# Scale factors in single columns and on ScalarE, scores of two heads in a row, and a new plan in a fused attention and two-layer kernel

## The chip, the core and the metric

The kernel runs on one core of a Trainium2 chip. A core has five engines with instruction streams of their own: TensorE (PE, matrix products), VectorE (DVE), ScalarE (ACT), GpSimd (POOL) and SyncE (SP, which issues the transfers). The metric is the device time in microseconds (us); less is better.

## The reference

Attention over 4 batches, 8 heads, 576 positions and 64 values a head, in which a score counts only if it lies within tau of its row's maximum. Its output, 2304 tokens of 512 values, goes through two layers of 2048 hidden values with different activations.

```
scores = scale * q @ k.T
thresh = max(scores, axis=-1) - tau
scores = where(scores >= thresh, scores, -1e9)
attn = exp(scores - max(scores)); attn = attn / (sum(attn) + 1e-9)
x = (attn @ v).transpose(0, 2, 1, 3).reshape(2304, 512)
h = x @ w1_in;  g = h * tanh(log(1 + exp(h)));            x = g @ w1_out
h = x @ w2_in;  g = h * clip(h + 3, 0, 6) / 6;            out = g @ w2_out
```

## The kernel before

**Numbers in two halves.** Products are made in f16 from a high and a low half of each scaled f32 number. A matrix of weights comes as 64-bit words, in eight groups. `convert` takes a group through a chain: shifts and additions that make f32 (L566 on ACT, L574 on POOL or L576 on DVE, L582 and L587 on DVE), a maximum over the group, `group_scale` (L457 to L464, one column for each group: the power of two by which it is divided) and, after all groups, `summary` (L481 to L505: the inverse scales of several groups at once, two or eight columns wide). The sums that make low halves are lines of `sub`, L390, on DVE or POOL. A maximum over partitions (`spread`) goes through a diagonal matrix (L417 on ACT, L419 on DVE), a matmul (L422) and a maximum (L425).

**Attention.** For each pair of heads and each 128 queries, PE makes two rows of scores (s_s, L1471, on half of its rows, 64*128, in two banks), DVE their maximum (L1480), ACT the exponential (e_ex, L1490), DVE the mask (L1493), ACT and POOL the two halves p_h and p_lo (L1498, L390), a transfer transposes them, and PE multiplies by v (L1519). k is scaled at the start by `k_scaled` (kd_lk, L1408, POOL). `to_x` puts the outputs into the order of tokens (L1633, L1639).

**First layer.** `inner` makes h for blocks of 256 tokens while attention goes on (L886, he_t copied out at L935 by ACT or L937 by DVE); `first_layer` reads it back, applies the activation (L972, L975 on ACT, L981 on DVE), and multiplies by w_out (L1001). `split_sums` scales and splits y (L692 is the maximum of a block's y, L773, L756, L762, sm_zmy and yl_zhy), which is stored and loaded again as x.

**Second layer.** `second_layer` takes nine blocks of 256 tokens. For each, a line for all blocks makes xscale (L1038) and hscales (L1039, eight columns, one for each group) on DVE. Then seven products of sums of blocks in place of eight (`product`, L1074) are combined (`keep` L1092 on ACT or DVE, `plus` L1102 on DVE), the activation is applied (L1155, L1161), the result is split in a high half (gs_h, L1171 on ACT) and a low half (L390, by half of the columns on DVE and POOL), and multiplied by w_out (L1221); L1261 and L1265 add the parts, and the result is stored.

**What sets the order.** The class `Plan` orders all of it when the program is built. A task has a cost on each engine that may do it, tasks it waits for, buffers out of rings of fixed size, and a due time (`prio`, from START, STEP and the other constants at the head of the file). `run` takes, at each step, the engine whose best candidate starts first; `_candidate` picks among those that can start about then. WHO says which engines may do which kind of task. The engines then carry out their instructions in that order.

Of the kernel before, what the change touches and what calls it, by code (L numbers as in the profile page):

```python
# [47 lines left out]
STEP = 2.707  # L48
START = 3.45
PV_OFF = 2.656  # L50
V_FIRST = -2.975
FIRST_AHEAD = 4.857
PREP_AHEAD = 4.509
CONV_STEP = 1.127
CONV_AT = 5.033
LATE_STEP = 3.262
OUT_STEP = 1.134
OUT_AT = 154.337
V_AHEAD = 5.112
# [122 lines left out]
class Plan:  # L182
# [46 lines left out]
    def _start(self, task, e):  # L229
# [18 lines left out]
        return max(t, self.clock[e])

    def _candidate(self, e):  # L250
# [94 lines left out]
def fused_kernel(ctx: ExitStack, tc, q, k, v, tau, w1i, w1o, w2i, w2o, out):  # L345
# [106 lines left out]
    def group_scale(task, name, m, i, ring, after):  # L452

        top, sc = wsc[m]["top"][:, i : i + 1], wsc[m]["sc"][:, i : i + 1]
# [15 lines left out]
        return task({"dve": 0.45}, factor, [a], [], "zf" + name)  # L470

    def summary(task, m, ring, after):
# [5 lines left out]
        def inverses(e, n):  # L478
            ts = nc.vector.tensor_scalar
            s, inv = w["s"][:, n], w["is"][:, n]  # L480
            ts(s, w["sc"][:, n], 1.875, None, ALU.mult)  # L481
# [1366 lines left out]
```

## Time and profile before

| what | us |
|---|---|
| runs | 1019.13, 1015.05, 1014.83 |
| median | 1015.05 |
| the profiled execution's own time | 1014.54 |
| its span | 1012.7 |
| PE busy | 935.0 (92%) |
| DVE busy | 784.3 (77%) |
| ACT busy | 645.8 (64%) |
| POOL busy | 531.1 (52%) |

The span is the time from the first to the last instruction on the core; the rest of the execution's time lies around it. Busy shares are means over stages that differ. The stages are: 0 to 25 us, loads and first scores; 25 to 150, attention with the conversion of the first weights; 150 to 425, attention with the first layer's h beside it; 425 to 646, the rest of the attention and the first layer; 646 to 676, the passage to the second layer; 676 to 986, the second layer; 986 to 1013, its end. [...]

### The profile page before, as it was taken

The page shows a single profiled execution, that of the slowest core. Times are in us where ns is not written, and L with a number is a line of the kernel's source. Part 1 is how long each engine was busy: PE and PEld are TensorE (multiplying, and loading weights), DVE is VectorE, ACT ScalarE, POOL GpSimd, SP SyncE. Part 2 cuts the span into 40 slices and gives each one's busy share as a digit, 9 for nine tenths or more (in the row PEclk, how much of TensorE's full clock was granted, in tenths as well). Part 3 has the DMA queues.
Part 4 walks back from the last instruction along what each step waited for, and adds up shares of the span by engine and source line. Part 5 has one row for each costly group of instructions (what it writes and reads, how often), then busy time and mean ns, then how long its engine had stood idle before and what let it go on. Part 6 is the DMA issues. An engine that isn't in the chain of part 4 may idle for free. (4 is left out here: it accounts for less than half of the span.)

```text
span 1012.7 us, 25942 instructions
## 1 busy us (share of the span) xinstructions
PE 935.0 (92%) x10776; PEld 803.2 (79%) x10776; DVE 784.3 (77%) x1466; ACT 645.8 (64%) x1029; POOL 531.1 (52%) x405
## 2 busy tenths in 40 slices
PE   3568679999999999999999999969999999999996
PEld 1446457777777777888888888869999999999986
DVE  6998899887878787668989989987746746746754
ACT  4667667888778878567776878545436536435542
POOL 5578675778656666523676567544124224213332
PEclk9878779999999999999999999979999999999999
DMA  9778989999999999885656567642101101101001
GB/s 316 168 188 206 220 213 213 230 241 225 209 231 211 251 209 231 200 314 181 217 207 217 194 225 245 244 188 74 59 1 59 59 2 59 59 2 58 23 3 42
DMA packets 201654, 164.48 MB, mean 162 GB/s; under 512 B 174144, under 2 KB 174656, under 8 KB 195136
## 3 DMA queue, kind: packets, MB, share of 16 engines
q1 hardware_dynamic: 201536, 162.82, 60.1%
q8 instruction: 85, 1.39, 0.6%
q14 instruction: 33, 0.27, 0.1%
HBM read 84.28 MB, written 36.04 MB: 119 GB/s over the span
## 5 line engine op out<-in xcount | busy, mean ns | idle before, releaser
L390 POOL TENSOR_TENSOR p_ph<-e_ex,p_ph 128x128 f16<-128x128 f32 (+3 forms) x160 | 192.6, 1226 | 97.5 <-issue 69.5
L390 POOL TENSOR_TENSOR gs_h<-g_ab,gs_h 128x896 f16<-128x896 f32 x36 | 96.3, 2691 | 219.7 <-ACT gs_h L1171 219.7
L1074 PEld LDWEIGHTS <-w__h 128*128 128x128 f16 x2016 | 157.9, 99 | 7.8 <-issue 7.0
L1221 PEld LDWEIGHTS <-gs_h 128*128 128x128 f16 x1512 | 146.6, 98 | 17.8 <-DVE out_va L1265 1.4
L1493 DVE SCALAR_TENSOR_TENSOR e_ex<-s_s,thr_th,e_ex 128x576 f32<-128x576 f32 x144 | 112.1, 812 | 21.8 <-ACT thr_th L1485 16.2
L1480 DVE TENSOR_REDUCE nm_pk<-s_s 128x1 f32<-128x576 f32 x144 | 105.8, 751 | 29.5 <-PE s_s L1471 28.9
L1471 PE MATMUL s_s<-kd_lk,qs_qp 64*128 64x288 f32 x480 | 93.8, 502 | 36.8 <-DVE e_ex L1493 24.1
L1490 ACT ACTIVATE e_ex<-s_s,nm_pk 128x576 f32<-128x576 f32 x144 | 103.8, 731 | 32.2 <-DVE nm_pk L1480 30.7
L1498 ACT ACTIVATE p_ph<-e_ex 128x576 f16<-128x576 f32 x144 | 94.7, 679 | 15.8 <-DVE e_ex L1493 13.9
L1074 PEld LDWEIGHTS <-w__u 128*128 128x128 f16 x1008 | 99.5, 99 | 1.3 <-issue 1.3
L1519 PEld LDWEIGHTS <-pt_tr 128*128 128x128 f16 x2016 | 82.5, 103 | 16.7 <-issue 8.0
L1471 PEld LDWEIGHTS s_s<-kd_lk,qs_qp 64*128 64x128 f32 x480 | 46.8, 215 | 58.9 <-issue 37.8
L1519 PE MATMUL aux_pv<-vh,pt_tr 128*128 128x65 f16 (+1 forms) x1296 | 87.5, 204 | 6.1 <-DMA pt_tr<-p_ph 6.1
L1171 ACT ACTIVATE gs_h<-g_ab 128x1792 f16<-128x1792 f32 x36 | 59.9, 1691 | 35.3 <-DVE g_ab L390 34.1
L1519 PE MATMUL aux_pv<-vl_vl,pt_tr 128*128 128x64 f16 x720 | 71.5, 204 | 0.0
L1155 ACT ACTIVATE g_ab<-g_ab,aux,hscales 128x512 f32<-128x512 f32 x72 | 54.2, 804 | 20.4 <-DVE g_ab L1102 20.4
L935 ACT ACTIVATE he_t<-h_g,hin 128x512 f32<-128x512 f32 x70 | 47.8, 683 | 28.0 <-PE h_g L886 22.6
L390 DVE TENSOR_TENSOR gs_h<-g_ab,gs_h 128x896 f16<-128x896 f32 x36 | 48.0, 1334 | 17.9 <-ACT gs_h L1171 17.9
L1102 DVE TENSOR_TENSOR g_ab<-h_g0d,s_ka 128x256 f32<-128x256 f32 x36 | 13.6, 420 | 59.1 <-PE h_g0d L1074 42.0
L981 DVE SCALAR_TENSOR_TENSOR gs_h<-hp_e,fscales,gs_h 128x512 f16<-128x512 f32 x72 | 51.9, 743 | 4.6 <-ACT gs_h L975 4.4
L972 ACT ACTIVATE hp_e<-hl_l 128x512 f32<-128x512 f32 x72 | 42.3, 596 | 20.5 <-DVE gs_h L981 20.1
L975 ACT ACTIVATE gs_h<-hp_e,fscales 128x512 f16<-128x512 f32 x72 | 47.4, 683 | 7.3 <-PE y_y L1001 6.6
(677 smaller groups left out, 2628.7 us busy)
## 6 DMA issues: line engine op xcount, KB each, us to landing
hd<-he_t SPq DMA_DIRECT2D x36, 512.0 KB, 3.6
hl_l<-hd SPq DMA_DIRECT2D x18, 1024.0 KB, 5.1
raw_lr<-in_moe_w_in SPq DMA_DIRECT2D x16, 1024.0 KB, 5.5
raw_lr<-in_moe_w_out SPq DMA_DIRECT2D x16, 1024.0 KB, 6.1
yd<-yl_zhy SPq DMA_DIRECT2D x9, 896.0 KB, 4.8
qs_qp<-in_q SPq DMA_DIRECT2D x11, 576.0 KB, 6.4
v_lv<-in_v SPq DMA_DIRECT2D x16, 320.0 KB, 4.0
kd_lk<-in_k SPq DMA_DIRECT2D x16, 288.0 KB, 4.9
```

The costliest lines, as they stand in the source:

```text
L390: engine[e].tensor_tensor(dst, a, b, ALU.subtract)
L981: nc.vector.scalar_tensor_tensor(s.tile[:, k, 1], g.tile.rearrange("p (a n) -> p a n", a=2), fs[:, fp : fp + 1], s.tile[:, k, 0], ALU.mult ...
L1074: mm(dst.tile[:, i * Q : (i + 1) * Q], wt[2][fp][wl].tile[:, right - 1, c * P : (c + 1) * P], x[xl].tile[:, c, left - 1], start=first and ...
L1155: nc.scalar.activation(g.tile[:, k, 4:8], g.tile[:, k, 0:4], AF.Relu, bias=wsc[2]["aux"][:, fp : fp + 1], scale=hscale[:, fp : fp + 1],)
L1171: nc.scalar.activation(part.tile[:, :, 0], g.tile[:, :, 1:], AF.Copy)
L1221: mm(region(p), part[:, gl, left - 1], wt[3][fp][wl].tile[:, right - 1], start=fp == n == 0 and spot(p)[1] == 0, stop=fp == NG - 1 and n == 2,
L1471: mm(s[j].tile[:, half, :HALF], lh[r], rh[r], start=m == 0, stop=m == len(terms) - 1,)
L1480: nc.vector.tensor_reduce(neg.tile[:, j : j + 1], sv(j), AX.XY, ALU.max, negate=True)
L1490: nc.scalar.activation(ev(j), sv(j), AF.Exp, bias=neg.tile[:, j : j + 1])
L1493: nc.vector.scalar_tensor_tensor(ev(j), sv(j), thr.tile[:, j : j + 1], ev(j), ALU.is_ge, ALU.mult)
L1498: nc.scalar.activation(p16.tile[:, js, :S], e_.tile[:, js], AF.Copy)
L1519: mm(ov[:, dst, :d], pt.tile[:, j, ch, :], part.tile[:, src, vc, :], start=i == j == ch == 0 and part is vh, stop=j == w - 1 and ch == 8, ...
```

## The change

The power of two of a group and its inverse are now both made in `group_scale`, in single columns (for the first matrix, m = 0); `summary` does seven groups early and the last one alone, and its last step is ScalarE's. In `second_layer` xscale and hscales are made for each block behind its first product, xscale on DVE and hscales on ACT. k is scaled on ACT. All low halves of the second layer's g (`o0` and `o1`) are on DVE, as are eight low halves of weights (`u20`) that were POOL's. In `Plan`, PE stays with scores if another score row can start within STAY, and from JOIN_FROM on the first of a pair's score rows waits until two banks are free soon (JOIN), so that both heads' rows stand together. Nearly all constants of the plan have new values.

```
-STEP = 2.707
-START = 3.45
+STEP = 2.83
+START = 11.118
...
-    "c20": ("dve",), "c21": ("pool", "dve"), "c30": ("pool",), "c31": ("dve",),
-    "q2": ("pool", "dve"), "q3": ("pool",), "u20": ("pool",), "u21": ("pool",),
-    "u30": ("pool",), "u31": ("pool", "dve"), "uy0": ("pool", "dve"), "uy1": ("dve",),
-    "kh": ("pool",), "vh": ("act",), "q": ("dve",), "o0": ("dve",), "o1": ("pool",),
+    "c20": ("dve",), "c21": ("pool",), "c30": ("pool", "dve"), "c31": ("pool", "dve"),
+    "q2": ("pool", "dve"), "q3": ("pool", "dve"), "u20": ("dve",), "u21": ("pool",),
+    "u30": ("pool",), "u31": ("pool",), "uy0": ("pool", "dve"), "uy1": ("pool", "dve"),
+    "kh": ("act",), "vh": ("act",), "vl": ("dve",), "q": ("dve",), "o0": ("dve",), "o1": ("dve",),
...
+JOIN = 2.418
+JOIN_FROM = 306.548
+STAY = 0.992
...
+        if e == "pe" and task.kind == "s" and task.name[-1] == "0" and self.clock[e] > JOIN_FROM:
+            both = task.bufs[0].ring.when(2)
+            if both is None:
+                return None
+            t = max(t, both - JOIN)
...
+        if e == "pe" and self.halves:
+            more = [(s, t) for s, t in found if t.kind == "s" and s <= self.clock[e] + STAY]
+            if more:
+                return min(more, key=lambda c: (c[0], c[1].prio))
...
-        top, sc = wsc[m]["top"][:, i : i + 1], wsc[m]["sc"][:, i : i + 1]
+        top, sc, inv = (wsc[m][k][:, i : i + 1] for k in ("top", "sc", "is"))
...
+            if m == 0:
+                nc.vector.tensor_scalar_mul(inv, sc, 2.0 ** -111)
             nc.vector.tensor_scalar_mul(sc, sc, 2.0 ** -112)
+            if m == 0:
+                nc.vector.tensor_scalar(
+                    bits(inv), bits(inv), 3, INF_BITS, ALU.logical_shift_left, ALU.bitwise_and
+                )
+                nc.vector.tensor_scalar(bits(inv), bits(inv), INF_BITS, None, ALU.bitwise_xor)
...
+        def apply(e):
+            nc.scalar.activation(w["f"], w["is"], AF.Copy, scale=w["c"][:, 1:2])
+
+        some = slice(0, NG - 1)
+        early = {0: 2.5, 1: 1.5, 2: 3.5, 3: 1.5}[m]
+        a = task({"dve": early}, lambda e: part(e, some), after[:-1], [], f"zi{m}")
+        a = task({"dve": 1.0 if m % 2 else 1.6}, largest, [a, after[-1]], [], f"zs{m}")
         if m == 0:
-            step = NG // len(scaled_parts)
-            for i in range(len(scaled_parts)):
-                n = slice(i * step, (i + 1) * step)
-                scaled_parts[i] = task(
-                    {"dve": 0.7}, lambda e, n=n: inverses(e, n), after[n], [], f"zi{i}_"
-                )
-            return task({"dve": 1.6}, scales, [*after, *scaled_parts], [], f"zs{m}")
-        if m % 2 == 0:
-            return task({"dve": 2.4}, scales, after, [], f"zs{m}")
-        a = task({"dve": 0.9}, scales, after, [], f"zs{m}")
-        a = spread(task, f"s{m}", lambda: w["c"][:, 0:1], [], ring, a)
-        return task({"dve": 0.4}, rows, [a], [], f"zr{m}")
+            return a
+        if m % 2:
+            a = spread(task, f"s{m}", lambda: w["c"][:, 0:1], [], ring, a)
+            a = task({"dve": 0.31}, row_scale, [a], [], f"zr{m}")
+        return task({"act": 0.29}, apply, [a], [], f"zu{m}")
...
-            nc.vector.tensor_scalar(hscale, wsc[2]["b"], a, None, ALU.mult)
+
+        def hidden(e):
+            nc.scalar.activation(hscale, wsc[2]["b"], AF.Copy, scale=xs(blk, 0))
...
-        scaled = task({"dve": 0.4}, scales, [y_stored[blk], scaled_by["y"]], [], "zx")
-        gs, made = [], []
+        gs, made, scaled = [], [], []
...
             p1 = product(X, 1, 2, True, [], "a")
+            if u == 0:
+                a = task(
+                    {"dve": 0.16}, scales, [y_stored[blk], scaled_by["y"]], [], "zx", 0.0, 0, [p1]
+                )
+                scaled.append(a)
+                scaled.append(task({"act": 0.29}, hidden, [a], [], "zw", 0.0, 0))
...
-        kl = prep(pick("kh", act=0.65, pool=1.0), k_scaled, [lk], [kd], "kh")
+        kl = prep(pick("kh", act=0.72, pool=1.73), k_scaled, [lk], [kd], "kh")
...
-        mul(w["f"], w["f"], wsc[3]["f"], ALU.mult)
-        ts(w["f"], w["f"], 0.125, None, ALU.mult)
+        nc.vector.scalar_tensor_tensor(
+            w["f"], w["f"], 0.125, wsc[3]["f"], ALU.mult, ALU.mult
+        )
```

The order of VectorE at the passage to the second layer, before (sm_zmy0_8 is the maximum of the last block's y, hscales and xscale those of the second layer's blocks); three more pairs of L1038 and L1039 stand behind these rows:

```order
L1039 TENSOR_SCALAR hscales_126<-b2_6625,xscale_121 128x8
L692 TENSOR_REDUCE sm_zmy0_8_0_8_1_9780<-y_y00_0_0_8_0_9477 128x1
L695 TENSOR_SCALAR sm_zmy0_8_0_8_1_9780<-sm_zmy0_8_0_8_1_9780 128x1
L1038 TENSOR_SCALAR xscale_121<-xscale_121,xinv_122,scy_127 128x1
L1039 TENSOR_SCALAR hscales_126<-b2_6625,xscale_121 128x8
```

And now (L720, L723 are L692, L695 of before; L431 is the diagonal on DVE, L437 the maximum behind the matmul, L801 and L402 a part and a low half of the y of the block before):

```order
L801 SCALAR_TENSOR_TENSOR xf_zvy0_7_0_7_1_9687<-y_y00_0_0_7_0_9218,sm_zmy0_7_0_7_1_9528,xf_zvy0_7_0_7_1_9687 128x2x128 x3
L1009 SCALAR_TENSOR_TENSOR gs_h4_0_8_1_9532<-hp_e7_0_8_1_9703,fscales_125,gs_h4_0_8_1_9532 128x512
L801 SCALAR_TENSOR_TENSOR xf_zvy0_7_0_7_1_9687<-y_y00_0_0_7_0_9218,sm_zmy0_7_0_7_1_9528,xf_zvy0_7_0_7_1_9687 128x2x128
L402 TENSOR_TENSOR yl_zhy0_7_0_7_1_9741<-xf_zvy0_7_0_7_1_9687,yl_zhy0_7_0_7_1_9741 128x896
L1066 TENSOR_SCALAR xscale_121<-xscale_121,xinv_122,scy_127 128x1
L1284 TENSOR_SCALAR xscale_121<-xscale_121,scy_127 128x1
L720 TENSOR_REDUCE sm_zmy0_8_0_8_1_9830<-y_y00_0_0_8_0_9515 128x1
L723 TENSOR_SCALAR sm_zmy0_8_0_8_1_9830<-sm_zmy0_8_0_8_1_9830 128x1
L431 TENSOR_SCALAR dgb_zdy0_8_0_8_1_9862<-ident_75,sm_zmy0_8_0_8_1_9830 128x128
L437 TENSOR_REDUCE sm_zmy0_8_0_8_1_9830<-h_zpy0_8_0_8_1_9864 128x1
```

The operations on eight columns are gone from here, one xscale is left, and the chain of the last block's y stands in a row.

The order of VectorE in the early attention, where the second group of the first matrix gets its scale (sc0 the power of two, s0 and is0 the inverse), before:

```order
L460 TENSOR_SCALAR top0_146<-top0_146 128x1
L461 TENSOR_SCALAR sc0_147<-top0_146 128x1
L464 TENSOR_SCALAR sc0_147<-sc0_147 128x1
L1480 TENSOR_REDUCE nm_pk2_0_0_1_375<-s_s2_0_1_0_364 128x1
L481 TENSOR_SCALAR s0_148<-sc0_147 128x2
L482 TENSOR_SCALAR s0_148<-s0_148 128x2
L483 TENSOR_SCALAR is0_149<-s0_148 128x2
L484 TENSOR_SCALAR is0_149<-is0_149 128x2
```

And now, for the first group:

```order
L472 TENSOR_SCALAR top0_146<-top0_146 128x1
L473 TENSOR_SCALAR sc0_147<-top0_146 128x1
L477 TENSOR_SCALAR is0_149<-sc0_147 128x1
L478 TENSOR_SCALAR sc0_147<-sc0_147 128x1
L480 TENSOR_SCALAR is0_149<-is0_149 128x1
L483 TENSOR_SCALAR is0_149<-is0_149 128x1
L469 TENSOR_SCALAR top0_146<-top0_146 128x1
```

The four operations on two columns, which stood behind each second group, have gone; each group has three more on one column.

The order of PE at one query tile late in the attention (s_s14_0_0 and s_s14_0_1 are the score rows of the two heads), before:

```order
L886 LDWEIGHTS w0__h0_0__1_541
L886 MATMUL h_g00_0_0_5_1_5059<-x_fl8_2_2_4293,w0__h0_0__1_541 128x256
L1471 MATMUL s_s14_0_0_0_5064<-kd_lk14_0_4709,qs_qp14_0_4482 128x288 x2
L1639 MATMUL aux_fl11_4_1_5069<-istack_91,xtail1_144 128x64
L1471 MATMUL s_s14_0_1_0_5074<-kd_lk14_0_4709,qs_qp14_0_4482 128x288 x2
L1519 LDWEIGHTS pt_tr12_0_1_1_4945
L1519 MATMUL aux_pv12_0_0_1_5081<-vh0_134,pt_tr12_0_1_1_4945 128x65
```

And now:

```order
L914 LDWEIGHTS w0__h0_6__1_1470
L914 MATMUL h_g60_0_0_4_1_4999<-x_fl8_0_2_3618,w0__h0_6__1_1470 128x256
L1517 MATMUL s_s14_0_0_0_5076<-kd_lk14_0_4689,qs_qp14_0_4541 128x288 x2
L1517 MATMUL s_s14_0_1_0_5085<-kd_lk14_0_4689,qs_qp14_0_4541 128x288 x2
L1565 LDWEIGHTS pt_tr12_1_1_1_4983
L1565 MATMUL aux_pv12_0_0_1_5022<-vh0_134,pt_tr12_1_1_1_4983 128x65
L1565 LDWEIGHTS pt_tr12_1_1_1_4983
```

Before, a matmul that turns attention's output (L1639) stood between the two heads' scores; now they stand together. Over the whole program the stretches of score matmuls that stand in a row fall from 96 to 79.

## Rows read from the trace of the kernel before

**Rows 1.** Busy time of the engines by stage; columns: stretch, length, busy time (instructions), clock
```profile
25.00:150.00 125.00, 88.91 (x852) 63.65 (x852) 113.26 (x211) 82.91 (x146) 91.84 (x80) 0.79 0.83 199
...
425.00:646.00 221.00, 219.58 (x2018) 196.43 (x2017) 191.69 (x323) 164.69 (x243) 126.46 (x92) 1.00 0.64 225
646.00:676.00 30.00, 20.89 (x222) 19.03 (x220) 27.06 (x62) 10.03 (x14) 14.91 (x11) 0.83 0.58 217
676.00:986.00 310.00, 309.20 (x4253) 293.77 (x4250) 199.89 (x409) 150.91 (x197) 93.67 (x35) 1.00 0.12 40
```

**Rows 2.** What TensorE waited for, 0 to 150 us: total, times, longest
```profile
PE s_s L1471 <- DVE e_ex L1493: 25.8, 13, 5.2
...
PE s_s L1471 <- POOL kd_lk L1408: 7.0, 1, 7.0
```

**Rows 3.** VectorE in order of time, 33 to 38 us: start, length, operation
```profile
34.50 0.96 DVE L483 TENSOR_SCALAR is<-s 128x2 uint32<-128x2 uint32 x1
```

**Rows 4.** GpSimd in order of time, at 33 and at 665 us
```profile
33.39 2.05 POOL L574 TENSOR_TENSOR cvt_c__1_373<-cvt_c__1_373,eight 128x512 int32<-128x512 int32 x2
...
665.43 1.89 POOL L390 TENSOR_TENSOR yl_zhy<-xf_zvy,yl_zhy 128x896 f16<-128x896 f32 x1
```

**Rows 5.** Groups of instructions by shape, the whole span: busy, mean ns, idle before
```profile
L390 DVE TENSOR_TENSOR gs_h<-g_ab,gs_h 128x896 f16<-128x896 f32 x36 | 48.0, 1334 | 17.9 <-ACT gs_h L1171 17.9
...
L482 DVE TENSOR_SCALAR s<-s 128x2 uint32<-128x2 uint32 x4 | 3.2, 804 | 0.1
...
L481 DVE TENSOR_SCALAR s<-sc 128x2 f32<-128x2 f32 x4 | 2.0, 512 | 0.0
...
L460 DVE TENSOR_SCALAR top<-top 128x1 f32<-128x1 f32 x32 | 4.7, 148 | 0.4
...
L390 POOL TENSOR_TENSOR gs_h<-g_ab,gs_h 128x896 f16<-128x896 f32 x36 | 96.3, 2691 | 219.7 <-ACT gs_h L1171 219.7
...
L1408 POOL TENSOR_SCALAR kd_lk<-kd_lk,qscale 128x576 f32<-128x576 f32 x16 | 27.6, 1728 | 8.2 <-DMA kd_lk<-in_k 8.1
...
L1498 ACT ACTIVATE p_ph<-e_ex 128x576 f16<-128x576 f32 x144 | 94.7, 679 | 15.8 <-DVE e_ex L1493 13.9
...
L1102 DVE TENSOR_TENSOR g_ab<-h_g0d,s_ka 128x256 f32<-128x256 f32 x36 | 13.6, 420 | 59.1 <-PE h_g0d L1074 42.0
```

**Rows 6.** TensorE in order of time, 299.5 to 305.5 us
```profile
299.84 0.76 PE L1471 MATMUL s_s<-kd_lk,qs_qp 64*128 64x288 f32 x4
300.53 1.27 PE L886 MATMUL h_g<-x_fl,w__h__1_629 128*128 128x256 f16 x10
...
302.87 1.73 PE L1471 MATMUL s_s<-kd_lk,qs_qp 64*128 64x288 f32 x12
```

**Rows 7.** Busy time of the engines, 666 to 676 us
```profile
666.00:676.00 10.00, 6.79 (x72) 6.48 (x71) 8.22 (x24) 3.12 (x5) 3.40 (x2) 0.55 0.74 275
```

**Rows 8.** VectorE in order of time, 660.5 to 673 us
```profile
660.19 1.08 DVE L390 TENSOR_TENSOR yl_zhy<-xf_zvy,yl_zhy 128x896 f16<-128x896 f32 x1
...
663.93 1.21 DVE L692 TENSOR_REDUCE sm_zmy<-y_y 128x1 f32<-128x1024 f32 x1
...
665.55 1.79 DVE L1039 TENSOR_SCALAR hscales<-b,xscale 128x8 f32<-128x8 f32 x1
...
671.74 0.28 DVE L425 TENSOR_REDUCE sm_zmy<-h_zpy 128x1 f32<-128x128 f32 x1
```

**Rows 9.** What TensorE waited for, 646 to 676 us
```profile
PE h_zpy L422 <- ACT dgb_zdy L417: 3.4, 1, 3.4
PE h_g0d L1074 <- DVE sm_zmy L425: 2.0, 1, 2.0
```

**Rows 10.** VectorE's groups of instructions by shape, 425 to 646 us
```profile
L390 DVE TENSOR_TENSOR yl_zhy<-xf_zvy,yl_zhy 128x896 f16<-128x896 f32 x11 | 17.7, 1619 | 1.5 <-ACT yl_zhy L762 1.5
...
L576 DVE TENSOR_SCALAR cvt_c__1_9549<-cvt_c__1_9549 128x512 uint32<-128x512 uint32 x1 | 0.4, 420 | 0.0
```

More of the change, by code (lines that the diff above doesn't have):

```diff
@@ L46 @@
 RELEASE = dict.fromkeys(("s", "m", "h", "y", "aux"), 0.27)
-STEP = 2.707
-START = 3.45
[L50 to L59, printed above, removed]
+STEP = 2.83
+START = 11.118
+PV_OFF = 3.414
+V_FIRST = 5.763
+FIRST_AHEAD = 6.308
+PREP_AHEAD = 4.584
+CONV_STEP = 1
+CONV_AT = 6.827
+LATE_STEP = 1.5
+OUT_STEP = 4.268
+OUT_AT = 107.984
+V_AHEAD = 4.249
 MOE_OFF = 9.75
-MOE_LAG = 11.98
-RATE = 0.9
+MOE_LAG = 13.564
+RATE = 0.918
 NX = 3
-FLIP = 2.992
-ALPHA = {"act": 6.104, "pe": 4.357}
-FITS = 0.072
+FLIP = 3.534
+ALPHA = {"act": 5.473, "pe": 1.636}
+FITS = 0.168
 PORT = ("vl", "c", "u", "o", "zs", "q", "p")
@@ L469, in group_scale @@
             a = spread(task, name, lambda: top, [], ring, a)
[L470 removed]
+        return task({"dve": 0.97 if m == 0 else 0.5}, factor, [a], [], "zf" + name)
     def summary(task, m, ring, after):
@@ L480, in inverses, with bounds, part, largest @@
             s, inv = w["s"][:, n], w["is"][:, n]
-            ts(s, w["sc"][:, n], 1.875, None, ALU.mult)
+            ts(s, w["sc"][:, n], 2.0, None, ALU.mult)
             ts(bits(s), bits(s), 3, INF_BITS, ALU.logical_shift_left, ALU.bitwise_and)
             ts(bits(inv), bits(s), INF_BITS, None, ALU.bitwise_xor)
-            ts(inv, inv, 0.5, None, ALU.mult)
-        def scales(e):
+        def bounds(e, n):
             ts, tt = nc.vector.tensor_scalar, nc.vector.tensor_tensor
-            if m:
-                inverses(e, slice(0, NG))
+            bound = w["b"][:, n]
+            tt(bound, w["top"][:, n], w["sc"][:, n], ALU.mult)
+            ts(bits(bound), bits(bound), 3, INF_BITS, ALU.logical_shift_left, ALU.bitwise_and)
+            tt(bound, bound, w["is"][:, n], ALU.mult)
+        def part(e, n):
+            if m:
+                inverses(e, n)
+            if m % 2 == 0:
+                bounds(e, n)
+        def largest(e):
+            ts = nc.vector.tensor_scalar
+            part(e, slice(NG - 1, NG))
+            nc.vector.tensor_reduce(w["c"][:, 0:1], w["is" if m % 2 else "b"], AX.X, ALU.max)
             if m % 2:
-                nc.vector.tensor_reduce(w["c"][:, 0:1], w["is"], AX.X, ALU.max)
                 return
-            tt(w["b"], w["top"], w["sc"], ALU.mult)
-            ts(bits(w["b"]), bits(w["b"]), 3, INF_BITS, ALU.logical_shift_left, ALU.bitwise_and)
-            tt(w["b"], w["b"], w["is"], ALU.mult)
-            nc.vector.tensor_reduce(w["c"][:, 0:1], w["b"], AX.X, ALU.max)
             ts(bits(w["c"][:, 1:2]), bits(w["c"][:, 0:1]), INF_BITS, None, ALU.bitwise_xor)
@@ L554, in convert @@
             one_conversion(m, g, raw, [loaded, factors[g]], task)
+        if m == 0:
+            step = NG // len(scaled_parts)
+            scaled_parts[:] = [factors[i : i + step] for i in range(0, NG, step)]
         scaled_by[m] = summary(tasker(prio + 2 * NG * off), m, ring, factors)
@@ L849, in input_scales @@
             n = slice(part * NG // parts, (part + 1) * NG // parts)
-            after = scaled_parts[part : part + 1] if i == 0 else scaled_parts
+            after = scaled_parts[part] if i == 0 else [f for fs in scaled_parts for f in fs]
             a.append(task({"act": 0.27}, lambda e, n=n: scales(e, n), [ready, *after], [], f"zx0_{i}"))
@@ L1249, in factor_out @@
             nc.vector.tensor_scalar(xs(blk, 1), xs(blk, 0), const_y[:, 1:2], None, ALU.mult)
-        factored = task({"dve": 0.15}, factor_out, [scaled, scaled_by["out"]], [], "zo")
+        factored = task({"dve": 0.15}, factor_out, [*scaled, scaled_by["out"]], [], "zo", 0.0, NG - 1)
         side_, yo = Buf(r_out), Buf(r_out)
```

43 lines of the change are left out of this document (25 added, 18 removed).

## The prediction

> **What bounds the kernel now.** I read the stages first, then the waits of TensorE (PE), then the rows at the stalls. The profiled execution took 1014.54 us with a span of 1012.7, so 1.8 us lie around the span; the median of the runs, 1015.05, is 0.5 above it. In [rows 1] the reader is to compare PE's busy time with the length of each stage. From 425 to 646 (the rest of the attention and the first layer) PE is idle for 1.4 of 221 us, from 676 to 986 (second layer) for 0.8 of 310, at clock 1.00. There only less PE work helps. PE has room in two places: from 25 to 150, where it is idle for 36.1 of 125 us at a mean granted clock of 0.79, and from 646 to 676, the passage from layer one to layer two, where it is idle for 9.1 of 30 us at 0.83. The waits tell whom it waits for. Early it is VectorE (DVE): 25.8 us in thirteen waits for the masked exponentials (e_ex), and 7.0 us once for the first scaled k from GpSimd (POOL) [rows 2]. DVE is busy for 113.3 of those 125 us, 91%: its own work is what ends last, and any microsecond taken off it there can reach PE.
>
> Why DVE is so full shows in [rows 3, 4]: L483 handles two columns, 256 numbers, and takes 0.96 us. It ends at 35.46, and the pair of POOL additions that ran beside it ends at 35.44. L1039 (eight columns) starts at 665.55 and lasts 1.79, to 667.34; POOL's sum beside it runs to 667.32 [rows 4, 8]. So these small operations of several columns last until POOL's instruction is over. Single columns do not: L460, one column, means 148 ns over 32 instances [rows 5].
>
> **The passage.** In [rows 8] the reader is to see DVE's order from 663 on: L692 (the maximum of the last token block's y), then L1039 of the other blocks, one of them with 1.79 us, and only at 671.74 L425, which ends the maximum over partitions of that block's y. PE's waits there include 3.4 us for the diagonal dgb_zdy made from L692's result, and 2.0 us for L425 [rows 9]. [...]
>
> **The change, part by part.** The sum is against 1014.54.
>
> *A. Early stage, −4.8.* Removed: four sets of L481 to L484 on two columns, 16 operations; L481 sums to 2.0 us and L482 to 3.2 [rows 5], and L483 and L484 read like L482, in all 11.6 us. Added: three single columns for each of eight groups, 24 operations; at the pitch of about 0.19 us that such operations have in a row (an estimate from L460's 148 ns and a little issue time) 4.6 us. DVE saves 7.0 us. PE waits for e_ex for 23.5 of its 36.1 idle us in this stage, and some of DVE's work stands where nobody waits, so I take 55%, 3.8 us. The first k goes to ScalarE (ACT): L1408 takes 1728 ns on POOL; on ACT nothing of this shape was traced, the nearest row is L1498 with 576 columns, 0.68 us [rows 5]. That is 1.05 us earlier at the very start, where PE waits for it; I take 1.0. Fifteen more k add some 10 us to ACT over the attention, beside DVE's 91%. The new times by which work is due (first constants of the table) reorder everything else in this stage; bounds 0 and −8 (all of 7.0 and 1.05).
>
> [...]
>
> *B. Scores in a row, −2.7.* Score matmuls use half the rows (64*128), all others 128*128. Four of them start at 299.84 and the next other matmul at 300.53; twelve last 1.73 and four 0.76 [rows 6]. So one record costs (1.73−0.76)/8 = 0.121 us, and a stretch of them (0.69−0.48) = 0.21 beyond its records. In the order of the program the stretches fall from 96 to 79; 13 of the missing ones are in the time when PE is never idle. 13 × 0.21 = 2.7. Bounds: −3.8 with 0.08 more on entering, and +3.4 if sixteen newly joined pairs each hold PE back 0.21 us until the second bank is free.
>
> *C. Passage, −10.5.* No L1039 is left on DVE. A block's xscale (one column) is made behind that block's first products, its eight hidden scales on ACT. In the new order L720 (L692 before) follows the first block's xscale directly, and its diagonal is made on DVE behind it, with no queue. What is late next is the chain itself: maximum 1.21 and L437's 0.28 [rows 8], the diagonal on 128 columns (by the 1.08 us for 896 columns it takes at most that) and the hops between them, about 3 us. PE's order has two other products ahead of its matmul. I leave 1.5 us, half of the chain, for it and for the load of the x columns. Bounds −6 (part of the clock loss stays) and −12.
>
> *D. First layer, +1.5.* DVE takes eight low halves of weights (128x768, from POOL) and five more he_t copies, and gives eight shifts (L576) to POOL. An operation of two inputs on 128x896 takes 1.08 us undisturbed [rows 8], so 768 columns take 0.93: 7.4. Five copies at 0.68 (ACT's row for 576 columns, the nearest) are 3.4. Eight shifts at 0.42 [rows 10] are −3.4. DVE goes from 191.7 to about 199 of 221 us. PE idles 1.4 us with DVE at 87%, so I take a fifth, 1.5. Bounds: 0, and +11.7 if all of 7.4 reaches PE and every low half is stretched by 0.54 as the yl_zhy of this stage are (1.62 against 1.08) [rows 8, 10].
>
> *E. Second layer, 0.* All 36 low halves that POOL did in 2.69 us go to DVE (1.08 undisturbed, 1.33 mean) [rows 5]. DVE rises from 199.9 by at least 38.9 to 239 of 310 us. PE's operand is ready 1.4 us earlier. What hides it is DVE's idle time: ahead of L1102 alone 59.1 us over 36, 1.64 each, 42.0 of it spent waiting for PE's own products [rows 5]. If that cover is gone, each costs up to 1.08. Bounds 0 and +5.
>
> The other edits (one operation instead of two for the combined scales, seven columns early and one late for each weight's sums, f on ACT, factor_out by block) are short operations off PE's path in [rows 1]'s full stages, except at the passage, where C has them: 0.
>
> Sum: −4.8 −2.7 −10.5 +1.5 +0 = −16.5, to 998.0; with the 0.5 between this execution and the median, **998.5**.
>
> **Rivals.**
> R1, *only the passage is gained.* PE's early idle time is bound by the order of the chain score, peak, exponent, mask rather than by DVE's total, and the joined scores move waits about. For it: the single longest waits for e_ex last 5.2 us [rows 2], more than any L48x. Against: 91% busy. A and B are nothing: −10.5+1.5 = −9.0, 1006.
>
> R2, *DVE becomes the bound of the first layer.* For it: yl_zhy is already stretched by half [rows 10]. Against: POOL has less to do afterwards. D at its upper bound: −16.5−1.5+11.7 = −6.3, 1008.7. [...]
>
> R3, *the other side: the low halves on DVE hold PE's evacuations.* In the second layer PE's banks are emptied by DVE and ACT; a low half of 1.08 us ahead of L1131 (L1102 before) delays g, the activation and the next output. Full price 36 × 1.08 = 38.9: 1037. It makes the kernel slower than before by over 0.5% once more than 21.6 of the 38.9 us (0.6 us each) land on PE. For it: PE has no idle time there, so every delay shows. Against: 1.64 us idle ahead of each L1102.
>
> R4, *the passage still stalls.* The chain of the last block's y stays late because the operations of the block before (L801, L402) stand ahead of its maximum on DVE, and the clock falls again. C is nothing: −6.0, 1009.
>
> **How the numbers follow.** The forecast case (990 to 1003.5) has 0.45; R1 0.18; R2 0.10; R4 0.12; R3 0.11; better than 990, 0.04. The low end of the range is A, B and C at their bounds, −8 −3.8 −12, with D 0: 990.7, taken as 990. The high end takes in R1, R2 and most of R4: 1011; R3, the tail under 990 and a part of R4 are left out, 2 in 10. The measurement can tell about 0.5%, 5 us, from no change: to 1010.0 is faster. All of the forecast case, R1, the tail, and nearly all of R2 and half of R4 are faster: 0.78. The rest of R4 and R2, and half-strength R3, are the same: 0.12. R3 beyond 0.6 us each is slower: 0.10.
>
> **What would show it.** A: PE idle from 25 to 150 near 31 us, waits for e_ex about 21 to 22 us; the new single columns at 0.15 us beside POOL's work. B: fewer and longer score stretches, PE busy 2 to 3 us less in 150 to 646. C: no DVE operation of eight columns in the passage, PE idle below 2 us in the 30 us around it, mean granted clock there above 0.95. D: PE idle in the first layer about 3 us. E: PE busy in every slice of the second layer, DVE near 235 to 240. I am wrong if idle time from 25 to 150 stays at 36 (R1), if PE waits for gs_h or h_g there (R2), if waits on DVE appear in the second layer (R3), or if dgb_zdy or sm_zmy still lead the waits of the passage (R4).

## The result and the profile after

The changed kernel took 991.62 us (median of 990.03, 990.23, 993.0 and 994.76) against 1015.52 us for the kernel before in the same comparison: ratio 0.9761, 95% interval 0.9725 to 0.9798. That is 23.9 us less; 17 were forecast, in a range that holds 991.62 near its low end. The profiled execution (990.03, the fastest of the four) has a span of 988.3 us, 24.4 less than before.

Busy time by stage of the changed kernel, columns as in [rows 1]; the clock is the granted one of PE as a share of its full speed. A stage of the same name now holds later work, since everything stands some 11 to 24 us earlier:

```profile
25.00:150.00 125.00, 91.79 (x929) 64.40 (x925) 114.76 (x237) 93.99 (x167) 90.84 (x82) 0.84 0.92 221
425.00:646.00 221.00, 220.02 (x2035) 197.24 (x2033) 195.26 (x340) 162.77 (x243) 143.00 (x101) 1.00 0.64 229
646.00:676.00 30.00, 30.00 (x504) 29.57 (x502) 25.17 (x57) 18.68 (x26) 2.54 (x2) 1.00 0.49 177
```

From 646 to 676 PE is now full at clock 1.00, and so it is in the 30 us around its own passage (632.6 to 662.6); before, the passage had 9.1 us idle at 0.83, and from 666 to 676 PE was busy for 6.79 us at a mean clock of 0.55 [rows 7]. By an estimate from these two numbers, 6.79 × 0.45, some 3 us of them are the clock's, which with the idle time makes about 12 us. From 25 to 150 PE is still idle for 33.2 us, but it carries out 929 instructions instead of 852, at 0.84 instead of 0.79. In the second layer (the same length of 310 us, 18 us earlier) GpSimd does nothing and VectorE about 30 us more:

```profile
658.00:968.00 310.00, 308.67 (x4193) 292.71 (x4191) 229.84 (x459) 152.42 (x205) 0.00 (x0) 1.00 0.12 39
```

Where the time came from is read from PE's milestones. Of the kernel before, the last product of the attention and the first of the second layer:

```profile
422.88 0.40 PE L1519 MATMUL aux_pv<-vh,pt_tr 128*128 128x130 f16 x4
...
658.34 0.22 PE L1074 MATMUL h_g0a<-xl_x__1_0_0_9309,w__h 128*128 128x128 f16 x1
```

And of the changed kernel:

```profile
411.67 0.40 PE L1565 MATMUL aux_pv<-vh,pt_tr 128*128 128x130 f16 x4
...
644.91 0.22 PE L1103 MATMUL h_g0a<-xl_x__1_0_0_9351,w__h 128*128 128x128 f16 x1
```

The attention ends 11.2 us earlier; up to the first product of the second layer it is 13.4 us. Between these two marks PE carries out the same 384 products of h and 1728 of y in both kernels. The ends differ by 24.4, and behind the start of the second layer nothing more is gained or lost: from the 303rd of its products to the end both kernels take 326.4 us. So, in these two executions: attention −11.2, first layer −2.2, passage −11.0, second layer 0.

VectorE at the passage, changed kernel (the answer to [rows 8]):

```profile
633.06 1.22 DVE L615 SCALAR_TENSOR_TENSOR cvt_c__1_9458<-raw_lr,cvt_c__1_9458 128x1024 uint32<-128x1024 uint32 x1
...
643.04 0.21 DVE L1284 TENSOR_SCALAR xscale<-xscale,scy 128x1 f32<-128x1 f32 x1
645.11 1.22 DVE L720 TENSOR_REDUCE sm_zmy<-y_y 128x1 f32<-128x1024 f32 x1 [1.85 <-PE y_y L1029]
...
646.56 0.29 DVE L431 TENSOR_SCALAR dgb_zdy<-ident,sm_zmy 128x128 bf16<-128x128 f32 x1
647.85 0.29 DVE L437 TENSOR_REDUCE sm_zmy<-h_zpy 128x1 f32<-128x128 f32 x1 [1.00 <-PE h_zpy L434]
```

The last conversion of weights (L615) is over at 634.28, 10.6 us ahead of the first product. L720, the maximum of the last block's y, waits for nothing but PE, and L437 ends 3.0 us behind its start; it was 8.1 us, from 663.93 to 672.02 [rows 8].

What PE waits for up to 150 us, and the operations that the change made (the answers to [rows 2, 5]; the last two rows are ScalarE's):

```profile
PE s_s L1517 <- DVE e_ex L1539: 34.5, 19, 5.5
PE s_s L1517 <- ACT kd_lk L1441: 5.8, 1, 5.8
```

```profile
L402 DVE TENSOR_TENSOR gs_h<-g_ab,gs_h 128x896 f16<-128x896 f32 x72 | 74.4, 1087 | 15.6 <-ACT gs_h L1206 15.6
...
L502 DVE TENSOR_SCALAR is<-s 128x7 uint32<-128x7 uint32 x3 | 2.3, 756 | 0.1
...
L477 DVE TENSOR_SCALAR is<-sc 128x1 f32<-128x1 f32 x8 | 1.2, 154 | 0.3
...
L1441 ACT ACTIVATE kd_lk<-kd_lk,qscale 128x576 f32<-128x576 f32 x16 | 12.3, 771 | 4.2 <-DMA kd_lk<-in_k 4.1
...
L1069 ACT ACTIVATE hscales<-b,xscale 128x8 f32<-128x8 f32 x9 | 2.6, 292 | 0.4 <-DVE xscale L1066 0.4
```

The eight single columns of L477 take 153 to 156 ns, and each of them began while GpSimd was at work; seven columns (L502) take 756 on average. The low halves of g take 1.09 us on VectorE now that GpSimd does nothing beside them; those of [rows 5] took 1.33, and with GpSimd back on half of them (a_lo_on_pool, below) VectorE's half takes 1.52.

### The profile page after: what moved, and what is told of

It is laid out like the page before. It is cut to its first block, busy times and chain, and to the rows that moved or that the text cites. A ratio compares the mean times of both kernels' runs of the same rounds, so it can differ in the third digit from the quotient of the medians.

```text
span 988.3 us, 25879 instructions
## 1 busy us (share of the span) xinstructions
PE 921.7 (93%) x10776; PEld 796.0 (81%) x10776; DVE 790.4 (80%) x1512; ACT 651.6 (66%) x1054; POOL 407.4 (41%) x354
## 4 chain that ended last, share of the span: by engine, by line
PE 69%; DMA 5%; DVE 2%; issue 1%; ACT 0%; SPq 0%; DVEq 0%; ACTq 0%
PE y_y L1029 17%; PE h_g L914 11%; PE hp_g1a L1103 5%; PE h_g0a L1103 5%; DMA pt_tr<-p_ph 4%; PE s_s L1517 3%; PE aux_pv L1565 3%; PE hp_g1d L1103 2%; PE h_g0d L1103 2%; PE h_g1b L1103 1%; PE hp_g0b L1103 1%; PE y_y__1_8_0_15084 L1256 1%; PE y_y___1_0_0_10340 L1256 1%; PE y_y___1_7_0_14653 L1256 1%; PE y_y___1_6_0_13984 L1256 1%; PE y_y___1_5_0_13325 L1256 1%
## 5 line engine op out<-in xcount | busy, mean ns | idle before, releaser
L402 POOL TENSOR_TENSOR p_ph<-e_ex,p_ph 128x128 f16<-128x128 f32 (+3 forms) x160 | 189.0, 1203 | 119.6 <-issue 72.0
L1517 PE MATMUL s_s<-kd_lk,qs_qp 64*128 64x288 f32 x480 | 88.2, 480 | 41.7 <-DVE e_ex L1539 32.2
L1539 DVE SCALAR_TENSOR_TENSOR e_ex<-s_s,thr_th,e_ex 128x576 f32<-128x576 f32 x144 | 112.0, 811 | 15.1 <-ACT thr_th L1531 12.8
L1565 PEld LDWEIGHTS <-pt_tr 128*128 128x128 f16 x2016 | 80.4, 102 | 18.8 <-DMA pt_tr<-p_ph 10.4
L402 DVE TENSOR_TENSOR gs_h<-g_ab,gs_h 128x896 f16<-128x896 f32 x72 | 74.4, 1087 | 15.6 <-ACT gs_h L1206 15.6
L963 ACT ACTIVATE he_t<-h_g,hin 128x512 f32<-128x512 f32 x65 | 44.4, 684 | 22.7 <-PE h_g L914 15.5
L1196 DVE SCALAR_TENSOR_TENSOR g_ab<-g_ab,f 128x512 f32<-128x512 f32 x72 | 51.2, 747 | 5.0 <-ACT g_ab L1190 5.0
L1121 ACT ACTIVATE s_ka<-h_g0a 128x512 f32<-128x512 f32 x27 | 16.1, 596 | 49.5 <-PE h_g0a L1103 49.3
```

What stands on the lines that cost most here:

```text
L402: engine[e].tensor_tensor(dst, a, b, ALU.subtract)
L1517: mm(s[j].tile[:, half, :HALF], lh[r], rh[r], start=m == 0, stop=m == len(terms) - 1,)
L1539: nc.vector.scalar_tensor_tensor(ev(j), sv(j), thr.tile[:, j : j + 1], ev(j), ALU.is_ge, ALU.mult)
L1565: mm(ov[:, dst, :d], pt.tile[:, j, ch, :], part.tile[:, src, vc, :], start=i == j == ch == 0 and part is vh, stop=j == w - 1 and ch == 8, ...
```

## Experiments

Kernels whose name begins with b are the kernel before with an edit, those with a the changed one. Where it says that the order is kept, every engine has its instructions in the same order but for the edited ones. Each was timed against the kernel before; the changed kernel stands at 0.9761 on this scale, and 0.001 is 1.0 us.

**b_hscales_act.** The eight-column scales on ScalarE, where they stood.
```
-            nc.vector.tensor_scalar(hscale, wsc[2]["b"], a, None, ALU.mult)
+            nc.scalar.activation(hscale, wsc[2]["b"], AF.Copy, scale=a)
```


> The kernel before, its order kept; only the eight-column hscales of each second-layer block are made on ScalarE instead of VectorE, at the same place. My account (the queue of L1039 ahead of and behind the last block's maximum is the passage's stall): the passage gains most of its 12 us, so 8 to 11 us less in all. Rival (the order by block, not the engine, removed the stall, since the scales still all stand early and wait on the stores): 0 to 3 us less.


Measured 0.9973 (0.9960 to 0.9986), 2.7 us less: the rival's number, for another reason than its. Its waits of PE in the passage, and ScalarE's order there:

```profile
PE h_g0a L1074 <- ACT s_ka L1092: 3.1, 1, 3.1
...
PE h_zpy L422 <- ACT dgb_zdy L417: 0.9, 1, 0.9
```

```profile
663.18 0.66 ACT L1039 ACTIVATE hscales<-b,xscale 128x8 f32<-128x8 f32 x3
665.01 1.06 ACT L642 ACTIVATE st_h<-sum_h 128x1024 f16<-128x1024 f32 x1 [1.17 <-POOL sum_h L390]
665.97 0.58 ACT L1092 ACTIVATE s_ka<-h_g0a 128x512 f32<-128x512 f32 x1
```

The wait for dgb_zdy fell from 3.4 to 0.9 us, as my account had it, but the wait for the first copy of the second layer (s_ka) grew from 1.2 to 3.1 us. The copy starts at 665.97, behind the high half of the last group of weights (L642), which GpSimd's sum held until 665.01.

**b_hscales_by_block.** As above, and the scales of blocks 1 to 8 only ahead of each block's first activation.
```
-            nc.scalar.activation(hscale, wsc[2]["b"], AF.Copy, scale=a)
+            todo.append(lambda: nc.scalar.activation(hscale, wsc[2]["b"], AF.Copy, scale=a))
+            if blk == 0:
+                todo.pop()()
...
                 def relu(e, k=k, fp=fp):
+                    while todo:
+                        todo.pop()()
```


> The kernel before, its order kept, hscales on ScalarE and those of blocks 1 to 8 only ahead of each block's first activation (L1155), as the change does. If eight small operations in ScalarE's queue are what held the first copy of the second layer: 3 us less than b_hscales_act, 0.994. If the last weights' conversion holds it: the same as b_hscales_act, 0.997.


Measured 0.9975 (0.9958 to 0.9992), as b_hscales_act, and the wait for the copy is still there:

```profile
PE h_g0a L1078 <- ACT s_ka L1096: 3.4, 1, 3.4
```

So it is not the number of scales in ScalarE's queue that holds it, and the order by block, the rival of the run before, adds nothing here.

**b_hscales_act_keep_dve.** As b_hscales_act, the first copy on VectorE.
```
-                    if e == "act":
+                    if e == "act" and (blk, u, tag) != (0, 0, "a"):
```


> The kernel before, its order kept, hscales on ScalarE as in b_hscales_act, and the copy of the first product of the second layer (s_ka, L1092) on VectorE instead of ScalarE. In b_hscales_act PE still waited 3.1 us for that copy, which stood behind the high half of the last group of weights (L642), itself held until 665.01 by GpSimd's sum. If late conversions of weights are what remains of the passage's stall: 3 to 6 us less than b_hscales_act, ratio to the kernel before 0.991 to 0.994. Rival (something else is next, the last block's maximum or the x columns): no further gain, 0.997.


Measured 0.9953 (0.9933 to 0.9973), 4.7 us less than before and 2 less than b_hscales_act; the intervals overlap, and the time lies between the two accounts. In its trace PE is busy for all of the 10 us from 666 to 676 at clock 1.00, but later it waits 2.5 us for x columns of the next block:

```profile
PE h_g0a L1074 <- DMA xl_x__1_1_0_10071<-yd: 2.5, 1, 2.5
```

**b_single_columns.** The inverse scales of the first matrix column by column, 32 operations for 16; the order is kept.
```
+            for k in range(n.start, n.stop) if m == 0 else (n,):
+                c = slice(k, k + 1) if m == 0 else k
-            s, inv = w["s"][:, n], w["is"][:, n]
+                s, inv = w["s"][:, c], w["is"][:, c]
...
```


> The kernel before, its order kept; only the four inverse scales of the first matrix are made column by column (32 operations on one column for 16 on two). My account: VectorE saves about 5.5 us (11.6 less 32 times 0.19) between 25 and 150 us and PE gains about half, 3 us. Rival (VectorE's total is not what sets the pace there, the new order is): 0 to 1 us.


Measured 0.9921 (0.9908 to 0.9934): 8.0 us less (6.7 to 9.3), more than either account. The 16 operations took 11.5 us; 32 at the pace of b_three_edits below (eight in 1.25 us) take 5.0, so VectorE saves some 6.5 us by this estimate.

**b_k_on_act.** k on ScalarE; the order is kept.
```
-            if e == "act":
-                nc.scalar.activation(kd.tile, kd.tile, AF.Copy, scale=qscale)
-            else:
-                nc.gpsimd.tensor_scalar(kd.tile, kd.tile, qscale, None, ALU.mult)
+            nc.scalar.activation(kd.tile, kd.tile, AF.Copy, scale=qscale)
```


> The kernel before, its order kept; only k is scaled on ScalarE instead of GpSimd. My account: 1.0 us less at the start, nothing after, since ScalarE has room. Rival: ScalarE's queue delays exponentials early and up to 3 us are lost again.


Measured 0.9990 (0.9972 to 1.0009), not told from nothing. Its waits say why: the wait for k is 1.2 us shorter than in [rows 2], and the next, for the scale of v, which was 5.2 us, is 1.0 us longer.

```profile
PE s_s L1468 <- DVE vs_ve L1356: 6.2, 1, 6.2
PE s_s L1468 <- ACT kd_lk L1405: 5.8, 1, 5.8
```

**b_three_edits.** b_hscales_act, b_single_columns and b_k_on_act together.


> The three edits above together in the order of before. If they add up by my account: 12 to 15 us less, more than half of the 24 us that the change brought. If the new plan is what gained: under 6 us.


Measured 0.9891 (0.9873 to 0.9910): 11.1 us less, nearly half of what the change brought; alone the three make 2.7 + 8.0 + 1.0 = 11.7. What a column count does is best seen at one place of the traces. VectorE of the kernel before, and PE's next scores:

```profile
101.71 0.68 DVE L481 TENSOR_SCALAR s<-sc 128x2 f32<-128x2 f32 x1
102.42 1.08 DVE L482 TENSOR_SCALAR s<-s 128x2 uint32<-128x2 uint32 x1
103.54 1.08 DVE L483 TENSOR_SCALAR is<-s 128x2 uint32<-128x2 uint32 x1
104.66 0.96 DVE L484 TENSOR_SCALAR is<-is 128x2 f32<-128x2 f32 x1
105.53 1.53 DVE L1493 SCALAR_TENSOR_TENSOR e_ex<-s_s,thr_th,e_ex 128x576 f32<-128x576 f32 x2
```

```profile
106.48 3.25 PE L1471 MATMUL s_s<-kd_lk,qs_qp 64*128 64x288 f32 x12 [3.51 <-DVE e_ex L1493]
```

VectorE of b_three_edits at the same place (first two and last of eight single columns, and the masks):

```profile
97.21 0.14 DVE L483 TENSOR_SCALAR s<-sc 128x1 f32<-128x1 f32 x1
97.38 0.15 DVE L484 TENSOR_SCALAR s<-s 128x1 uint32<-128x1 uint32 x1
...
98.38 0.15 DVE L486 TENSOR_SCALAR is<-is 128x1 f32<-128x1 f32 x1
98.46 1.53 DVE L1492 SCALAR_TENSOR_TENSOR e_ex<-s_s,thr_th,e_ex 128x576 f32<-128x576 f32 x2
```

Before, 3.8 us pass from L481 to the masks, and PE waits 3.51 us for them; its twelve score matmuls then take 3.25 us, against 1.73 for twelve in [rows 6]; the granted clock in these 3.2 us is 0.50. Now the eight operations take 1.25 us, and PE's wait for the masks at this place is gone. Over the first 150 us the waits for e_ex fall from the 25.8 us of [rows 2] to 14.8:

```profile
PE s_s L1470 <- DVE e_ex L1492: 14.8, 7, 3.6
```

**a_extra_two_columns** and **a_extra_one_column.** The changed kernel, order kept, with three more operations on a spare tile in each of eight group scales; their results are not used. Shown is the run with two columns; the other has `0:1` for `0:2`.
```
...
+                for k in range(3):
+                    nc.vector.tensor_scalar(
+                        bits(spare[:, 0:2, 0]), bits(spare[:, 0:2, 0]), INF_BITS, None, ALU.bitwise_xor
+                    )
```


> The changed kernel, its order kept, with three more operations on two columns of a spare tile in each group scale of the first matrix (24 in all; they compute nothing that is used). If two columns beside GpSimd's work cost 0.8 us each and all of it is on the path of the masks: 19 us slower than the changed kernel, more if the clock falls. If half of it is: 10 us. If the price of a column count is not what mattered: as with one column, below 3 us.

> The same with three more operations on one column of the spare tile (24 in all). At 0.19 us each VectorE has 4.6 us more: 2 to 5 us slower than the changed kernel if the path is VectorE's, near 0 if not.


Measured 0.9923 (0.9898 to 0.9949) and 0.9805 (0.9782 to 0.9827): 16.4 and 4.5 us over the changed kernel, 12.0 apart. The interval of the one-column run overlaps the changed kernel's, so its 4.5 us alone are not told from nothing. The groups of VectorE with two columns, then with one:

```profile
L488 DVE TENSOR_SCALAR spare<-spare 128x2 uint32<-128x2 uint32 x24 | 14.4, 602 | 0.6
```

```profile
L488 DVE TENSOR_SCALAR spare<-spare 128x1 uint32<-128x1 uint32 x24 | 3.6, 151 | 0.6
```

The second column costs VectorE 14.4 − 3.6 = 10.8 us, and the kernel 12.0, give or take some 3 by the two intervals. So these microseconds count about in full. The 602 ns are a mean over 24. How far such an operation depends on GpSimd shows in the kernel before, in its sixteen on two columns (L481 to L484): with GpSimd idle beside them three took 0.17 us each; of the thirteen with GpSimd at work eleven took 0.68 to 1.08, the other two 0.16 and 0.49.

**a_lo_on_pool.** The changed kernel, order kept, 36 low halves of g back on GpSimd.
```
-                sub(e, part.tile[:, k, 1], g.tile[:, k, 1:], part.tile[:, k, 0])
+                sub("pool" if k else e, part.tile[:, k, 1], g.tile[:, k, 1:], part.tile[:, k, 0])
```


> The changed kernel, its order kept, with the second low half of each pair in the second layer back on GpSimd (36 of 72). By term E nothing: within 1 us. If GpSimd's 2.7 us each delayed PE: several us slower.


Measured 0.9787 (0.9764 to 0.9810); the interval overlaps the changed kernel's, so no difference is shown. GpSimd takes 2.9 us for each, and PE waits for none of them. From the 303rd product of the second layer to the end its profiled execution takes as long as the changed kernel's, within 0.01 us:

```profile
L402 POOL TENSOR_TENSOR gs_h<-g_ab,gs_h 128x896 f16<-128x896 f32 x36 | 103.7, 2895 | 213.1 <-ACT gs_h L1206 199.0 <-PE y_y___1_7_1_14654 L1256 14.1
```

**a_no_join_no_stay** and **a_no_join.** The changed kernel, planned anew without both rules (STAY at −1e9, JOIN_FROM at 1e9), and without JOIN alone.
```
-JOIN_FROM = 306.548
-STAY = 0.992
+JOIN_FROM = 1e9
+STAY = -1e9
```


> The changed kernel, planned without the two rules that put scores together (JOIN and STAY off, all other numbers the same). By the forecast's term B it loses 2.7 us (ratio to the kernel before near 0.979). Rival: the joined scores bring nothing, since PE waited more in the attention after the change; then within 1 us of the changed kernel (0.976), or faster.


Measured 1.0045 (1.0026 to 1.0065): 29 us slower than the changed kernel, which neither account had. The longest waits of PE that the changed kernel does not have:

```profile
PE h_g0a L1103 <- DMA xl_x__1_0_0_9806<-yd: 9.3, 1, 9.3
PE aux_fl L1685 <- DVE xtail L1656: 8.2, 1, 8.2
```

The planner put the x columns and a turn of attention's output elsewhere. This prices the plan, not the scores: the run is no measure of term B. Nor does it bring the old order of scores back: in its trace they stand in 82 stretches, where the changed kernel has 79 and the kernel before 96.


> The changed kernel planned without JOIN alone; the order is the same up to the middle of the attention. By term B the rest of the attention is about 2 us longer up to the last score row. Rival: the joined rows gain nothing there, since the first row waits for the second bank as long as the stretches save; within 1 us at the last score row. What the plan does behind the attention (conversions, passage) may differ and is read apart.


Measured 0.9798 (0.9772 to 0.9824), 3.8 us over the changed kernel with overlapping intervals. In its profiled execution the last score row is 6.6 us later than in the changed kernel's, but 6.1 of them were there already at the first place where the orders differ (309.95 us against 303.8). Its scores stand in 79 stretches too, so the run does not test term B, which prices fewer stretches.

**b_three_edits_late_off.** b_three_edits with one number of the plan, which converts the last weights earlier.
```
-OFF_LATE = 1.875
+OFF_LATE = 4.862
```


> The kernel of b_three_edits with one number of the plan changed, OFF_LATE from 1.875 to 4.862 as in the changed kernel. The order is the same up to the start of the first layer; from there the last group of weights is converted earlier (17 VectorE rows ahead of the last block's maximum, before 6), the hidden scales are done before it, and no conversion is left in the passage. If the late conversions are the other part of the passage's 12 us: 6 to 8 us less than b_three_edits, ratio to the kernel before 0.981 to 0.983. If the earlier conversions cost the first layer what they give, or the passage has another stall: 0.987 to 0.990.


Measured 0.9948 (0.9931 to 0.9966), slower than b_three_edits by 5.8 us. That is worse than either account: the rival, too, expected no more than 0.990. My account was right on the place, the rival on where it would be lost. In its trace the first product of the second layer starts at 662.68, and the passage behind it is nearly full, at clock 1.00:

```profile
662.00:680.00 18.00, 17.62 (x309) 17.42 (x308) 9.30 (x24) 8.74 (x15) 1.16 (x1) 1.00 0.44 157
```

But PE's longest wait from 400 us on now stands in the first layer, for a block's scale (L697) at 619.83. On VectorE a conversion of 3.13 us, which GpSimd held back by 0.94, and more of the same group stand ahead of it:

```profile
PE y_y L1003 <- DVE sm_zmy L697: 6.8, 1, 6.8
```

```profile
611.83 3.13 DVE L584 SCALAR_TENSOR_TENSOR cvt_c__1_9126<-raw_lr,cvt_c__1_9126 128x1024 uint32<-128x1024 uint32 x1 [0.94 <-POOL cvt_c__1_9126 L576]
...
617.70 1.21 DVE L589 SCALAR_TENSOR_TENSOR cvt_c__1_9126<-raw_lr,cvt_c__1_9126 128x1024 uint32<-128x1024 uint32 x1
...
619.83 0.14 DVE L697 TENSOR_SCALAR sm_zmy<-sm_zmy 128x1 uint32<-128x1 uint32 x1
```

From the last product of the attention to the first of the second layer this kernel takes 242.4 us, where b_three_edits takes 234.5; of its start in the second layer it loses another 5, with PE waiting 3.1 us for low halves (gs_h).

## Why the prediction was right, and where it was off

The forecast time was 7 us too long, inside the range. In the two profiled executions the attention gained 11.2 us where A and B together had 7.5, the first layer gained 2.2 where D had a loss of 1.5, and the passage gained 11.0 where C had 10.5. So about half of what was missed is in the attention and half in the first layer. The measured 23.9 us is what the prediction adds up for its low end, A, B and C all at their bounds and D at nothing (−23.8); that end, 990.7, leaves out the 0.5 that the forecast itself adds. The parts named for "faster" add up to about 0.82, not 0.78.

**A, early stage: right in mechanism, mis-sized.** The step "I take 55%" failed. Single columns alone gave 8.0 us where the term had 3.8, and the pair of runs with extra operations shows the rate: 10.8 us of VectorE time cost 12.0, give or take 3. These operations stand in line ahead of masks for which PE waits, so they count about in full; at the place shown, the matmuls behind such a wait ran at a granted clock of 0.50 besides.

The sign that I named held only where the order is kept: there the waits for e_ex up to 150 us fell from 25.8 to 14.8 (b_three_edits). In the new plan they rose to 34.5 (from 25 to 150 alone, from 23.5 to 26.1), while those for xn_dn and for the scale of v, in the list from which [rows 2] are taken, all but went:

```profile
PE aux_fl L1633 <- DVE xn_dn L1596: 8.2, 3, 3.6
PE s_s L1471 <- DVE vs_ve L1356: 5.2, 1, 5.2
```

All of PE's waits in that list add up to 53.7 us before and 49.4 after; the sum tells, not a single line. From 25 to 150 PE idled 2.9 us less where 5 were expected; the rest of the gain shows as the higher granted clock (0.84 for 0.79). The 1.0 us of k is in PE's first wait (7.0 to 5.8), but alone it was handed to the next wait; that the changed kernel kept it, having no wait for the scale of v, is read from its trace and was not tried apart.

**B, scores in a row: right in size, its cause and what it is worth in the end not shown.** Score matmuls (the same count of 424 in 240 us, all but a trace of it at clock 1.00) of the kernel before, then of the changed one:

```profile
170.00:410.00 240.00, 69.72 (x424) 1.00 1.05 227
```

```profile
160.00:400.00 240.00, 66.83 (x424) 1.00 1.07 228
```

That is 2.9 us less, 2.7 were forecast. But from 150 to 425 the waits for transposed p went up, which the term did not have; before, changed, and a_lo_on_pool, which has the changed kernel's order here:

```profile
PE aux_pv L1519 <- DMA pt_tr<-p_ph: 3.0, 4, 1.1
```

```profile
PE aux_pv L1565 <- DMA pt_tr<-p_ph: 6.6, 7, 1.9
```

```profile
PE aux_pv L1565 <- DMA pt_tr<-p_ph: 3.6, 7, 0.9
```

Executions of one order differ by as much as the gain, so how much of it these waits take back is open, and so is what made them. Not the rules JOIN and STAY but other numbers of the plan brought most of the fall in stretches (96 to 82 without them).

**C, passage: right in size (−11.0 for −10.5), half right in mechanism, and in part by luck.** No run shows the 12 us that the term's bound takes for the passage: 9.1 of them are idle time [rows 1], the other 3 an estimate from the mean clock of 0.55 [rows 7]; what the two executions show is a passage 11.0 us shorter, full and at clock 1.00. From the first product of the second layer to the start of the 303rd, counted in the traces, PE takes 27.9 us in the kernel before, 25.3 in b_hscales_act, 24.3 in b_hscales_by_block and in b_three_edits, 24.0 with the copy on VectorE, 17.5 in b_three_edits_late_off and 16.9 in the changed kernel. The step that failed is the one that put the stall down to the queue of L1039 alone: taking that away gives about 3 us. Even this is not firm from these marks, since b_k_on_act, with the passage untouched, took 24.9 in its profiled execution, after a first layer 2.3 us longer (the timed 2.7 us, 1.4 to 4.1, are the better number). First layer and passage together are steadier: from the last product of the attention to that 303rd it is 263.2 us before, 262.5 in b_k_on_act, 259.8 in b_hscales_act, 258.8 in b_three_edits, 259.9 in b_three_edits_late_off and 250.0 in the changed kernel.

The other 7 us of the passage are the late conversion of the last weights, which stood in it too, on ScalarE and GpSimd, with the loads behind it. In [rows 9] the waits name dgb_zdy and L425, which ended last there. GpSimd's sum for the last high half ended at 665.47, just as the diagonal began (665.42), and the high half (L642) stood right behind the diagonal, with 1.2 us of waiting for s_ka to show for it; with the diagonal earlier this wait grew to 3.1. Converting earlier is not free: one number moved alone took 7 us off the passage and put more than that into the first layer and the second layer's start. Only the new plan as a whole has neither. The term had no conversion in it; that the new plan also moved it is why its number came out.

**D and E.** The first layer gained 2.2 us where 1.5 were to be lost: the step that failed is the fifth of VectorE's added work that was to reach PE. 1.4 us of the gain may be a wait for the diagonal of the last weights' scale, in the list from which [rows 9] are taken; it is gone where the conversion is earlier, which was read and not tried apart:

```profile
PE h_zps L422 <- ACT dgb_zds L417: 1.4, 1, 1.4
```

From 425 to 646 VectorE's load rose by 3.6 us (to 195.3 of 221) where 7.4 were counted, though the two windows do not hold quite the same work, and PE idled 1.0 us: at 88% VectorE does not hold PE there. The eight moved low halves took 1.08 us on average (0.95 to 1.40) where 0.93 were counted, so some were stretched as R2 had it, and PE did not pay for it. E is 0 as forecast; VectorE is at 74% (229.8 of 310; 239 forecast), and with half of the low halves on GpSimd at 2.9 us PE waits as little, so in this order the work is hidden on either engine and R3's price did not show. In another order it can: in b_three_edits_late_off PE waited 3.1 us for low halves.

**What stays open.** The three edits in the order of before make 11.1 of the 23.9 us. The other 12.8 came with the new plan and the edits that were not tried apart; 8.8 of them lie in the first layer and the passage (258.8 against 250.0), and which numbers of the plan made them is not shown.

## What to carry to other kernels

Price a small operation by what runs beside it and by what stands behind it in its queue: here a second column made it four times as long on average (602 against 151 ns) with GpSimd's work beside it, and in line ahead of the operation that TensorE waits for that time counted about in full (10.8 us of it for 12.0). When a stall has two causes that end near each other, removing the one that the waits name shows the other, so ask of each stall what ends next. A plan of tuned numbers fits one set of rules and costs: changing one rule or number of it measures the plan, not the rule.

## What the runs showed of the hardware

Two columns against one for the same operation in the early stage: 602 against 151 ns on average over 24, with GpSimd busy for 78.3 and 89.5 of the 125 us from 25 to 150. Seven columns took 756 ns on average over three (L502 of the changed kernel). All of these read one tensor. L507 of the changed kernel reads two; its two instances on one column took 0.46 and 1.07 us and ended at 125.00 and 533.28, where GpSimd's work beside them ended at 124.98 and 533.26. The second of them:

```profile
532.21 1.07 DVE L507 TENSOR_TENSOR b<-top,sc 128x1 f32<-128x1 f32 x1
```

Executions of one order differ in the early attention. a_lo_on_pool has the order of the changed kernel until the second layer, yet from 25 to 150 us its profiled execution carried out 901 instead of 929 PE instructions, at a granted clock of 0.79 instead of 0.84:

```profile
25.00:150.00 125.00, 93.68 (x901) 65.09 (x898) 112.93 (x233) 90.74 (x161) 88.83 (x82) 0.79 0.91 215
```

At the end of the attention these two executions are 1.6 us apart. b_three_edits and b_three_edits_late_off, with one order up to there, are 8.2 us apart (last products at 412.1 and 420.3), with granted clocks of 0.85 and 0.81 from 25 to 150. So several microseconds of one execution there say nothing of the kernel: a difference of 3 us between kernels shows in a dozen timed runs, as for b_hscales_act, and not in a pair of traces.
